# Moving layer 2's logits steps one chunk ahead in the bodies of layer 1

## The chip, the cores and the metric

The kernel runs on one core of one Trainium2 chip. The metric is the device time of one launch in microseconds (us). The kernel before takes 1067.36 us, the median of three runs (1065.39 to 1070.98).

## What is computed

Three stages follow each other: chunked attention, a mixture of experts with normalised logits (layer 1), and a second mixture with a skip score (layer 2). Every token goes to its best expert alone.

```python
def _moe_ref(x, expert_emb, tau, w1, w2):          # layer 1
    logits = normalised(x) @ normalised(expert_emb).T / tau
    expert_idx = argmax(logits, axis=1)
    gate_w = softmax(logits)[arange(N), expert_idx]
    for e in range(E):
        mask = expert_idx == e
        h = maximum(x[mask] @ w1[e], 0.0)
        out[mask] = gate_w[mask, None] * (h @ w2[e])

def _moe2_ref(x, w_skip, w_gate, w1, w2):          # layer 2
    do_compute = x @ w_skip > 0
    out = x.copy()
    xc = x[do_compute]
    logits = xc @ w_gate
    e_idx, gate_w = argmax(logits), softmax(logits) at the argmax
    y = the same experts' products on xc
    out[do_compute] = xc + y
```

There are 4608 tokens of 512 values, 8 experts and 1024 hidden values, all float32. The products are made of float32 values split in a high and a low part (fp32r): high times high, low times high, high times low.

## The kernel before

Attention (phase1) writes each token's row, with its gate and its number, to a place in DRAM sorted by expert. Layers 1 and 2 (moe) then run over these sorted rows. Their order is written out by hand, one instruction stream for each engine (functions sp, pe, act, dve, pool), and the engines meet at semaphores: take(e, s) waits until s has reached its count and counts it down again.

slots walks through the experts. A body works on one tile of rows: pair on 256 rows, single on 128, half on 64. The first body of an expert (first=True) is a pair in layer 1; it also converts the weights of the next expert: ScalarE casts a chunk of 512 KB to its high part (high, line 152), VectorE subtracts to the low part (split, line 155), and SP fetches the expert after that (fetch) into the staging tiles so freed. In layer 1 there are 18 pair bodies, eight of them firsts, and three bodies of single or half tiles; x < NE means layer 1.

A pair body on TensorE (pair in pe) has two products. Product one runs over eight chunks f of the hidden values; each chunk is 12 matmuls of 256 columns (line 795) into one of three PSUM tiles Hb and posts "h". ScalarE makes relu f out of it (HTh, line 1008, posts "hh"), VectorE the low half f (HTl, line 1212, posts "hl"). From the fourth chunk on TensorE waits for low half f - 3, whose tile Hb it writes again. Then TensorE transposes the next tile's X into XTp (xt, line 802), and product two runs in 16 steps of three matmuls of 512 columns into Yp; the first eight steps wait for the eight low halves in turn. ScalarE copies XTp to XTh, VectorE subtracts to XTl, SP loads the X after that, and ScalarE evicts Yp, scaled by the gate, into the tile y (yev).

The result y of a layer 1 body is the input of layer 2, so layer 2's logits are made from it inside the next body, in three steps between the chunks of product one (logits in pe). Step 0 waits for "yr" and transposes y into XTp (line 840, posts "yt"); ScalarE copies that to yT (line 984, posts "yT"). Step 1 multiplies yT with the gate's weights into a part of XTp (posts "lt"); ScalarE copies it to ls (line 986, posts "lS"). Step 2 sums the parts into lgp, again in XTp (posts "lg"). VectorE copies lgp to lgs (logits in dve, line 1105) and posts "lc". Since the transposes of the next X overwrite XTp, TensorE waits for lc ahead of them. "yr" is posted by VectorE's start of a body, which waits for "ys", the eviction of y by ScalarE, and copies the gate (line 1182). Behind f = 1 TensorE also makes the ranks (rk, line 192) of the tile whose logits were made a body before; ranked on VectorE reads them.

In the kernel before, TensorE's steps stand behind f = 2, 4 and 6, ScalarE's copies behind relu 2 and 4, and VectorE's copy behind low half 7. In first bodies ScalarE's casts stand behind relus 0, 1, 2, 3, 6 and 7 and at the body's end, and VectorE's splits behind low halves 1, 2, 3, 4 and 7 and after XTl.

Of the kernel before, what the change touches and what calls it, by code (L numbers as in the profile page):

```python
# [25 lines left out]
NE = 8  # L26
# [28 lines left out]
class Kernel:  # L55
# [556 lines left out]
    def moe(self, ctx):  # L612
# [178 lines left out]
        def pe(e):  # L791
# [69 lines left out]
            def pair(x, first=False):  # L861
                hi, lo = self.w[x % 2]
                begin(x, first)
                for f in range(KF):
                    if f >= 3:
                        e.wait_ge(sem["hl"], f - 2)
                    for i in range(3):
                        if f == 0 and i == 2:
                            take(e, "xl")
                        for k in range(KD):  # L870
                            r = mm(
                                Hb[f % 3][:, 0 : 2 * P].rearrange("p (a t) -> p a t", a=2), (hi, lo, hi)[i][:, k * FF + f * P : k * FF + (f + 1) * P],
                                (XTh, XTh, XTl)[i][:, k], i == 0 and k == 0, i == 2 and k == KD - 1,
                            )
                    r.then_inc(sem["h"], 1)
                    if f == 1 and x < NE and (x or not first):
                        rk()
                    if f in (2, 4, 6) and x < NE:
                        logits(f // 2 - 1)
                take(e, "xc")  # L880
                if x < NE:
                    take(e, "lc")
                xt()
                if first and x:
                    take(e, "wr2")
                mm2(x, 0, True)
                mm2(x, 1, False)
# [77 lines left out]
        def act(e):  # L965
            j = e.alloc_register("jac")
            s = nc.scalar

            def xh():
                take(e, "xt")  # L970
                s.copy(XTh, XTp).then_inc(sem["xh"], 1)

            highs = [0], [1], [2], [3], [], [], [4], [5], [6, 7]

            def high(x, r):
                if x <= LAST:
                    for c in r:
                        take(e, wf[c], 16)
                        self.split_hi(wcol(x, c)[0], c).then_inc(sem["wv"], 1)

            def logits(part):
                take(e, ("yt", "lt")[part])
                if part == 0:
                    s.copy(yT, XTp).then_inc(sem["yT"], 1)
                else:
                    s.copy(ls, lgq).then_inc(sem["lS"], 1)

            def rowcopy():
                take(e, "rf")
                s.copy(row[:, :, 0:DM], L[:, :, 0:DM]).then_inc(sem["rc"], 1)  # L990

            def expo():
                take(e, "nmx")
                for a in range(2):
                    s.activation(ex[:, a, :], lg[:, a, :], AF.Exp, bias=nm[:, a, :], accum_out=sm[:, a, :]).then_inc(
                        sem["sm"], 1
                    )

            def yev(a):
                take(e, "y")  # L1000
                r = s.activation(L[:, a, 0:DM], Yp[a], AF.Copy, scale=gt[:, a, :])  # L1001
                if a:
                    r.then_inc(sem["ys"], 1)

            def pair(x, first=False):
                for f in range(KF):
                    take(e, "h")
                    s.activation(HTh[:, f, :], Hb[f % 3][:, 0 : 2 * P], AF.Relu).then_inc(sem["hh"], 1)  # L1008
                    if f in (2, 4) and x < NE:
                        logits(f // 2 - 1)  # L1010
                    if first:
                        high(x + 1, highs[f])
                xh()
                if x < NE:
                    rowcopy()
                    expo()
                if first:
                    high(x + 1, highs[8])
                if x < NE:
                    e.drain()  # L1020
                    yev(0)
                    yev(1)

            def single(x, first=False, half=False):
                n = HP if half else P
                c = slice(0, n) if first else slice(P, P + n)
                if x < NE:
                    logits(0)
                if first:
                    high(x + 1, range(4))  # L1030
                for h in range(2):
                    take(e, "h")
                    s.activation(
                        Hs, Hb[h].rearrange("p (k f) -> p k f", k=4),
                        AF.Copy if half else AF.Relu,
                    ).then_inc(sem["r"], 1)
                    if h:
                        xh()
                    elif x < NE:
                        logits(1)  # L1040
                    take(e, "ht")
                    s.activation(
                        HTh[:, 4 * h : 4 * h + 4, c], (Hb[2], Hb[0])[h][:, 0 : 4 * n].rearrange("p (k f) -> p k f", k=4),
                        AF.Relu if half else AF.Copy,
                    ).then_inc(sem["hh"], 1)
                    if first and h:
                        high(x + 1, range(4, NCH))
                if x < NE:
                    rowcopy()
                    expo()  # L1050
                    e.drain()
                    if half:
                        take(e, "y")
                        s.activation(
                            L[0:HP, 1, 0:DM], Yp[1][0:HP, :], AF.Copy, scale=gt[0:HP, 1, :]
                        ).then_inc(sem["yb"], 1)
                    else:
                        yev(1)

            e.sem_inc(sem["ys"], 1)  # L1060
            for ph in range(2):
                expo()
                xh()
                slots(e, j, ph, pair, single, partial(single, half=True))
                if ph == 0:
                    for a in range(2):
                        take(e, "yt")
                        s.copy(yT[:, :, a, :], Hb[a].rearrange("p (k t) -> p k t", k=KD)).then_inc(sem["yT"], 1)

        def dve(e):  # L1070
# [145 lines left out]
            def pair(x, first=False):  # L1216
                start(x)
                for f in range(KF):
                    take(e, "hh")
                    low(f, Hb[f % 3][:, 0 : 2 * P])  # L1220
                    if f == 1 and x < NE and (x or not first):
                        ranked()
                    if first and f in (1, 2, 3, 4, 7):
                        split(e, x + 1, [min(f - 1, 4)])
                if x < NE:
                    logits()
                xl()
                if x < NE:
                    gating_a()
                    if first:  # L1230
                        split(e, x + 1, [5])
                    gating_b()
                    xc([1])
                    clear()
                    if first:
                        split(e, x + 1, [6, 7])
                else:
                    e.drain()
                    xc(range(2))
                    if first:  # L1240
                        split(e, x + 1, [5, 6, 7])
                    finals(range(2))

            def single(x, first=False, half=False):
# [5 lines left out]
                if x < NE:  # L1250
                    v.tensor_copy(t0[:, 0, :], self.bigi)
                    ranked()
                elif first:
                    split(e, x + 1, range(2))
                for h in range(2):
                    if h and x < NE:
                        logits()
                    take(e, "hh")
                    a = slice(4 * h, 4 * h + 4)
                    src, high = (Hb[2], Hb[0])[h][:, 0 : 4 * n].rearrange("p (k f) -> p k f", k=4), HTh[:, a, c].bitcast(F32)  # L1260
                    if half:
                        r = v.scalar_tensor_tensor(
                            HTh[:, a, o + HP : o + P], in0=src, scalar=0.0, in1=high, op0=ALU.max, op1=ALU.subtract
                        )
                    else:
                        r = v.tensor_tensor(HTl[:, a, c], src, high, op=ALU.subtract)
                    r.then_inc(sem["hl"], 4)
                    if h == 0 and first:
                        split(e, x + 1, range(2, 4))
# [148 lines left out]
```

## Time and profile before

| | before |
|---|---|
| median of 3 runs | 1067.36 us |
| profiled execution | 1066.52 us |
| its span | 1064.8 us |
| TensorE matmul, busy | 950.7 us (89%) |
| VectorE, busy | 539.6 us (51%) |
| ScalarE, busy | 478.4 us (45%) |
| GpSimd, busy | 196.1 us (18%) |
[...]

The span reaches from the first to the last instruction; attention takes its first 221 us, layer 1 the stretch to 778 us, and layer 2 the rest. A matmul's row lasts from its start to its modelled end, and matmuls overlap, so the time that one takes from the stream is read from start to start. The number in brackets at the end of a row is the time that the engine sat idle before it, and what ended that; PEq, ACTq and DVEq are the engines' own queues, which stand at a semaphore.

### The profile page before, as it was taken

How to read it: one execution, taken by the hardware profiler on the slowest of the kernel's cores; microseconds unless marked ns; L12 is line 12 of the kernel's file. 1: busy time of each engine (PE TensorE's matmuls, PEld its weight loads, DVE VectorE, ACT ScalarE, POOL GpSimd, SP SyncE). 2: the span in 40 equal slices, each digit the busy share in tenths (PEclk: the TensorE clock that was granted, in tenths of full speed). 3: DMA queues.
4: the chain of work that ended last, by engine and by line, in shares of the span. 5: the costliest groups of instructions: out<-in, count | busy, mean ns of one | idle time of the engine just before them, and what ended most of it. 6: DMA issues, size and time to landing. Idle time of an engine off the chain costs nothing. (4 is left out here: it accounts for less than half of the span.)

```text
span 1064.8 us, 20672 instructions
## 1 busy us (share of the span) xinstructions
PE 950.7 (89%) x7136; PEld 823.6 (77%) x7136; DVE 539.6 (51%) x1569; ACT 478.4 (45%) x931; POOL 196.1 (18%) x251
## 2 busy tenths in 40 slices
PE   7978999889999969999999999999999975979797
PEld 6866877678878858888788887788889864769685
DVE  5878889753226345343432244263255544646252
ACT  4767877643336535253433344363333423434241
POOL 4044442411111211111111111111121000000001
PEclk9999899999999998999999999999999988889899
DMA  8989998770153461405111511510525656572512
GB/s 211 254 241 238 246 229 204 259 258 22 40 198 106 171 199 48 171 36 193 52 41 41 197 47 42 203 46 21 197 64 208 212 171 220 174 249 91 192 47 65
DMA packets 133642, 157.11 MB, mean 148 GB/s; under 512 B 50421, under 2 KB 87285, under 8 KB 133232
## 3 DMA queue, kind: packets, MB, share of 16 engines
q1 hardware_dynamic: 121888, 132.16, 40.8%
q0 software_dynamic: 11600, 22.99, 5.9%
q8 instruction: 85, 1.39, 0.6%
q14 instruction: 69, 0.57, 0.2%
HBM read 123.42 MB, written 51.12 MB: 164 GB/s over the span
## 5 line engine op out<-in xcount | busy, mean ns | idle before, releaser
L795 PE MATMUL Yp<-w_hi,HTh 128*128 128x512 f32 x464 | 189.3, 408 | 0.0
L795 PE MATMUL Yp<-w_lo,HTh 128*128 128x512 f32 x464 | 186.2, 401 | 0.0
L1008 ACT ACTIVATE HTh<-Hb 128x256 fp32r<-128x256 f32 x208 | 79.9, 384 | 232.4 <-ACTq L660 230.1
L795 PE MATMUL Yp<-w_hi,HTl 128*128 128x512 f32 x440 | 176.5, 401 | 0.0
L1212 DVE SCALAR_TENSOR_TENSOR HTl<-Hb,HTh 128x256 fp32r<-128x256 f32 x208 | 87.6, 423 | 173.6 <-DVEq L660 173.5
L795 PE MATMUL Hb<-XTx,w_hi 128*128 128x256 f32 x832 | 141.1, 292 | 21.9 <-PEq L660 19.2
L155 DVE TENSOR_TENSOR w_lo<-stg,w_hi 128x1024 fp32r<-128x1024 f32 x120 | 143.6, 1216 | 0.5 <-DVEq L660 0.4
L795 PEld LDWEIGHTS Hb<-XTx,w_hi 128*128 128x128 f32 x832 | 115.6, 192 | 33.8 <-issue 26.0
L795 PE MATMUL Hb<-XTx,w_lo 128*128 128x256 f32 x832 | 133.1, 283 | 0.0
L152 ACT CAST w_hi<-stg 128x1024 fp32r<-128x1024 f32 x128 | 130.9, 1044 | 4.7 <-ACTq L660 4.7
L795 PE MATMUL Hb<-XTl,w_hi 128*128 128x256 f32 x832 | 132.8, 282 | 0.1
L1327 POOL DMA_INDIRECT xs<-row,few_i x44 | 44.9, 1020 | 466.9 <-POOLq L660 459.4
L1327 POOL DMA_INDIRECT out<-row,few_i x63 | 69.2, 1099 | 254.8 <-POOLq L660 239.1
L795 PEld LDWEIGHTS Hb<-XTx,w_lo 128*128 128x128 f32 x832 | 114.1, 191 | 0.0
L795 PEld LDWEIGHTS Hb<-XTl,w_hi 128*128 128x128 f32 x832 | 113.6, 191 | 0.5 <-issue 0.5
L795 PEld LDWEIGHTS Yp<-w_hi,HTh 128*128 128x128 f32 x464 | 89.3, 192 | 20.0
L795 PEld LDWEIGHTS Yp<-w_lo,HTh 128*128 128x128 f32 x464 | 89.2, 192 | 20.0
L795 PEld LDWEIGHTS Yp<-w_hi,HTl 128*128 128x128 f32 x440 | 84.4, 192 | 20.4
L1001 ACT ACTIVATE y<-Yp,few_f 128x512 f32<-128x512 f32 x37 | 25.5, 688 | 113.4 <-ACTq L660 113.4
L1182 DVE COPY few_f<-few_f 128x2 f32<-128x2 f32 x32 | 5.8, 182 | 137.5 <-DVEq L660 110.9
L1093 DVE TENSOR_TENSOR XTl<-XTp,XTx 128x1024 fp32r<-128x1024 f32 x34 | 41.6, 1223 | 59.7 <-DVEq L660 59.6
L802 PE MATMUL XTp<-ident,X 128*128 128x128 f32 x272 | 37.4, 282 | 36.3 <-PEq L660 36.1
(207 smaller groups left out, 1311.0 us busy)
## 6 DMA issues: line engine op xcount, KB each, us to landing
stg<-in_moe_w SPq DMA_DIRECT2D x128, 512.0 KB, 6.5
X<-xs SPq DMA_DIRECT2D x34, 516.0 KB, 3.8
vbd<-in_v SPq DMA_DIRECT2D x144, 64.0 KB, 4.5
xs<-pad SPq DMA_DIRECT2D x16, 516.0 KB, 10.9
qs<-in_q SPq DMA_DIRECT2D x12, 512.0 KB, 5.0
ks<-in_k SPq DMA_DIRECT2D x12, 512.0 KB, 8.0
y<-xs SPq DMA_DIRECT2D x11, 512.0 KB, 4.2
xs<-pads SPq DMA_DIRECT2D x16, 258.0 KB, 4.6
```

The source lines that it names most:

```text
L152: return self.nc.scalar.copy(hi, self.stg[c % NSTG])
L155: return eng.tensor_tensor(lo, self.stg[c % NSTG], hi.bitcast(F32), op=ALU.subtract)
L795: return nc.tensor.matmul(out, lhsT=l, rhs=r, start=start, stop=stop)
L802: r = nc.tensor.transpose(XTp[:, k, a, :], X[:, a, k * P : (k + 1) * P], ident)
L1001: r = s.activation(L[:, a, 0:DM], Yp[a], AF.Copy, scale=gt[:, a, :])
L1008: s.activation(HTh[:, f, :], Hb[f % 3][:, 0 : 2 * P], AF.Relu).then_inc(sem["hh"], 1)
L1093: v.tensor_tensor(XTl, XTp, XTh.bitcast(F32), op=ALU.subtract).then_inc(sem["xl"], 1)
L1182: r = v.tensor_copy(gt, gtn)
L1212: v.scalar_tensor_tensor(HTl[:, f, :], in0=src, scalar=0.0, in1=HTh[:, f, :].bitcast(F32), op0=ALU.max, op1=ALU.subtract).then_inc(sem["hl ...
L1327: e.indirect_dma_start(out=dst, out_offset=bass.IndirectOffsetOnAxis(ap=idx, axis=0), in_=src, in_offset=None, bounds_check=bound - 1, oob ...
```

## The change

The three steps on TensorE move from behind f = 2, 4 and 6 to behind f = 1, 3 and 5 of product one; in f = 1 step 0 follows the ranks. ScalarE's two copies move from behind relus 2 and 4 to behind relus 1 and 3, ahead of the weight cast that stands there in first bodies. VectorE's copy moves from behind low half 7 to ahead of low half 6 in pairs. In single and half bodies VectorE's copy moves from between the two low halves to ahead of the first. No instruction is added or removed.

```diff
@@ pair in pe
                     if f == 1 and x < NE and (x or not first):
                         rk()
-                    if f in (2, 4, 6) and x < NE:
-                        logits(f // 2 - 1)
+                    if f in (1, 3, 5) and x < NE:
+                        logits(f // 2)
                 take(e, "xc")
@@ pair in act
                     s.activation(HTh[:, f, :], Hb[f % 3][:, 0 : 2 * P], AF.Relu).then_inc(sem["hh"], 1)
-                    if f in (2, 4) and x < NE:
-                        logits(f // 2 - 1)
+                    if f in (1, 3) and x < NE:
+                        logits(f // 2)
                     if first:
                         high(x + 1, highs[f])
@@ pair in dve
                 for f in range(KF):
+                    if f == KF - 2 and x < NE:
+                        logits()
                     take(e, "hh")
                     low(f, Hb[f % 3][:, 0 : 2 * P])
...
-                if x < NE:
-                    logits()
                 xl()
@@ single in dve
+                if x < NE:
+                    logits()
                 for h in range(2):
-                    if h and x < NE:
-                        logits()
                     take(e, "hh")
```

## Rows read from the trace of the kernel before

**Rows 1.** The page's first part: busy us (share of the span) and instructions, TensorE.

```profile
PE 950.7 (89%) x7136; PEld 823.6 (77%) x7136; DVE 539.6 (51%) x1569; ACT 478.4 (45%) x931; POOL 196.1 (18%) x251
```

**Rows 2.** Waits of TensorE, 221 to 778 us: line, releaser, total us, times, longest.

```profile
PE XTp L802 <- PEq L660: 35.4, 18, 2.6
PE Hb L795 <- PEq L660: 5.5, 1, 5.5
```

**Rows 3.** Timeline, end of product one, second body of an expert: start us, length us, instruction.

```profile
265.46 0.63 PE L795 MATMUL Hb<-XTl,w_hi 128*128 128x256 f32 x4
...
266.74 0.42 DVE L1212 SCALAR_TENSOR_TENSOR HTl<-Hb,HTh 128x256 fp32r<-128x256 f32 x1 [1.43 <-DVEq L660]
267.08 0.17 DVE L1105 COPY lgs<-XTp 128x18 f32<-128x18 f32 x1
...
267.55 1.07 PE L802 MATMUL XTp<-ident,X 128*128 128x128 f32 x8 [1.46 <-PEq L660]
```

**Rows 4.** Timeline, the same place in the first body of an expert.

```profile
377.44 0.63 PE L795 MATMUL Hb<-XTl,w_hi 128*128 128x256 f32 x4
...
379.06 1.22 DVE L155 TENSOR_TENSOR w_lo<-stg,w_hi 128x1024 fp32r<-128x1024 f32 x1
380.19 0.17 DVE L1105 COPY lgs<-XTp 128x18 f32<-128x18 f32 x1
...
380.66 1.06 PE L802 MATMUL XTp<-ident,X 128*128 128x128 f32 x8 [2.59 <-PEq L660]
```

**Rows 5.** Timeline of TensorE, the same place in a pair body of layer 2.

```profile
824.39 0.64 PE L795 MATMUL Hb<-XTl,w_hi 128*128 128x256 f32 x4
824.87 1.03 PE L802 MATMUL XTp<-ident,X 128*128 128x128 f32 x8
```

**Rows 6.** Timeline, product one of the body of rows 3: gate copy, ranks, logits steps.

```profile
253.51 0.17 DVE L1182 COPY few_f<-few_f 128x2 f32<-128x2 f32 x1 [5.68 <-DVEq L660]
...
255.23 0.19 PE L192 MATMUL Rp<-oh,ones 128*128 128x8 bf16 x2
...
260.58 0.64 PE L795 MATMUL XTp<-yT,wg 128*32 128x256 f32 x8
...
261.36 0.37 ACT L986 COPY yT<-XTp 128x256 f32<-128x256 f32 x1 [0.21 <-ACTq L660]
...
264.08 0.51 PE L795 MATMUL XTp<-sel,yT 128*128 128x9 f32 x4
```

**Rows 7.** Timeline, start of the body behind a half tile: gate copy and ranks.

```profile
322.48 0.17 DVE L1182 COPY few_f<-few_f 128x2 f32<-128x2 f32 x1 [0.20 <-DVEq L660]
...
323.31 0.19 PE L192 MATMUL Rp<-oh,ones 128*128 128x8 bf16 x2
```

**Rows 8.** Timeline of ScalarE in the first body of rows 4, behind relu 2.

```profile
369.97 1.02 ACT L984 COPY yT<-XTp 128x1024 f32<-128x1024 f32 x1 [0.48 <-ACTq L660]
370.88 1.05 ACT L152 CAST w_hi<-stg 128x1024 fp32r<-128x1024 f32 x1
371.83 0.38 ACT L1008 ACTIVATE HTh<-Hb 128x256 fp32r<-128x256 f32 x1
```

**Rows 9.** Loads of X: one issue on SP's timeline; issue to landing of 23 loads.

```profile
390.31 0.38 SPq L726 DMA_DIRECT2D X<-xs  x1
...
DMA to landing us min/median/max: 3.4/3.8/6.4
```

**Rows 10.** Windows of 12 us behind the wait: us, PE busy (matmuls), granted clock, DMA share, GB/s.

```profile
238.60:250.60 12.00, 11.94 (x49) 0.86 0.16 46
336.70:348.70 12.00, 11.95 (x56) 1.00 0.58 217
...
267.50:279.50 12.00, 11.95 (x56) 1.00 0.17 44
```

**Rows 11.** Timeline of TensorE, start of the expert behind one with a single body.

```profile
398.41 1.19 PE L795 MATMUL Hb<-XTx,w_hi 128*128 128x256 f32 x4 [5.47 <-PEq L660]
```

## The prediction

> (f counts the chunks of product one, its relus and its low halves from 0 to 7, as the code does.)
>
> **What bounds the kernel now.** I read the page's busy shares first, then who waited for whom on TensorE over layer 1, then the timeline of single bodies. TensorE is busy 89% of the span [rows 1]; no other engine passes 51% on the same page. Between 221 and 778 us, which is all of layer 1, TensorE has only two waits of weight: 35.4 us in 18 waits ahead of the transposes of the next X (line 802), and one of 5.5 us at the start of a product [rows 2]. Elsewhere in layer 1 its matmuls stand end to end. So a wait of TensorE that goes shortens the time, and a step on ScalarE or VectorE costs only what it makes TensorE wait.
>
> The 18 waits are one per pair body, and come in two sizes. In a body that isn't the first of its expert, the last four matmuls of product one start at 265.46. VectorE takes the last low half at 266.74, copies the logits at 267.08, and the transposes start at 267.55, 0.30 us after that copy ends (267.08 + 0.17) [rows 3]. In the first body of an expert a weight split of 1.22 us stands between low half and copy; the copy comes at 380.19, and the transposes at 380.66, again 0.30 us after its end [rows 4]. The releaser is in both cases "lc", which the logits copy posts: the transposes overwrite XTp, in which the logits stand. There are eight firsts (one per expert) and ten others: 8 x 2.6 + 10 x 1.46 = 35.4, which is the row of waits.
>
> **The change part by part.**
>
> *VectorE's copy moves from behind low half 7 (in firsts, also behind its split) to ahead of low half 6.* This takes relu 7, low half 7 and the split out of the chain that ends in lc. What remains for the transposes is xf (the next X in SBUF), xc and lc. A case with the first two alone is layer 2: its pair bodies have no logits, and there the transposes start 0.48 us after the last four matmuls start (824.39 to 824.87), with no wait [rows 5]. Against that spacing, the others lose 267.55 - 265.46 - 0.48 = 1.61 us each, the firsts 380.66 - 377.44 - 0.48 = 2.74 us. If lc is early: 10 x 1.61 + 8 x 2.74 = 16.1 + 21.9 = 38.0 us.
>
> *Is lc early?* The last logits matmuls now run behind f = 5, two chunks before the end of product one; a chunk is three runs of four matmuls at 0.48 [rows 5], so 1.4 us, and two are 2.8. Low half 5 should trail the end of its chunk as low half 7 does: that starts at 266.74 where the chunk's end is 265.46 + 0.48 = 265.94, so it ends (0.42 long) 1.2 us behind. The copy and its 0.30 of signal add 0.5: lc stands 1.7 us after f = 5, over 1 us before f = 7 ends. That is the cover in the others; in firsts the splits make VectorE run later or earlier by about half a microsecond. If it were gone, TensorE would wait in line 802 as now, by the difference. Low halves 6 and 7 slip by at most 0.17 us; product two needs low half 7 only at the eighth of its sixteen steps, some 5 of 12 us after the transposes begin [rows 10].
>
> *TensorE's transposes of y move ahead by a chunk.* They wait for "yr", posted by VectorE at the body's start behind the last eviction of the body before. The gate copy that posts it starts at 253.51 and ends at 253.68; TensorE is through the ranks at 255.42, where the transposes will stand [rows 6]. Margin 1.7, less 0.3 of signal: 1.4 us. The tightest body is that behind a half tile: copy at 322.48, ranks until 323.50 [rows 7], margin 0.5. I take 0; were the margin exceeded, everything in TensorE's queue would stand behind the wait.
>
> *ScalarE's two copies move with them*: yT at 1.0 us, ls at 0.37 [rows 6, 8]. The three steps stay two chunks apart, so TensorE finds yT and ls as early as now. In firsts the yT copy now stands between relu 1 and the cast of weight chunk 1, so relu 2 comes late: the pattern today is copy 369.97, cast 370.88, relu 371.83 [rows 8], which I put at half a microsecond's lag of relu 3, and the same lag would fall on relu 2. TensorE needs low half 2 before f = 5: two chunks of 1.4 and the logits matmuls of 0.6 [rows 6] after f = 2 ends, 3.4 us, against the usual 1.2 and the lag of 0.5. Cover 1.7 us; VectorE's split between is over by then, since it waits for relu 2 too. I take 0, with 0.5 x 8 = 4 us as bound.
>
> [...]
>
> *Single and half bodies* (three in layer 1): VectorE's logits copy goes ahead of low half 0 and swaps some 0.4 with 0.17 us beside TensorE's second half of product one; 0, with bounds of 0.4 each to both sides, 1.2 us in all. No DMA is moved, and neither SP's nor POOL's order changes. *X is there in time*: a load that SP issues as late as 390.31, behind the weight fetches, lands in 6.4 us at the longest [rows 9], before the body that needs it for its transposes even begins (398.41) [rows 11].
>
> *The clock.* In five of the eight firsts TensorE's granted clock falls after the wait: 0.86 over the 12 us behind it, against 1.00 in the other three firsts and behind the others' waits [rows 10]. [...] A fall costs 0.14 x 12 = 1.7 us by that row, or 7 matmuls fewer of 56, 7 / 56 x 12 = 1.5; I take 1.6, five are 8.0 us. With the wait gone I expect the falls gone: none stands behind a wait of 1.46, nor behind layer 2's transposes, which don't wait. Bounds 0 and 8.0.
>
> [...]
>
> The wait of 5.47 us at 398.41 [rows 11] stands at an expert's start, behind an expert with one body; no moved step releases it, and I leave it as it is.
>
> **Sum.** 38.0 + 8.0 = 46.0 us. The profiled execution took 1066.52 (span 1064.8), so 1020.5; the median shown is 0.84 higher, which gives 1021.4. I say 1021.
>
> **The rivals.**
> *The clock is not given back* (other short waits still let it fall): 38.0 alone, 1029.
> *A part of the wait stays in firsts*, because VectorE or ScalarE is late there: about a split of 1.22 us still ahead of lc, or relu 2 holding f = 5. 8 x 1.22 = 9.8 us less gives 1031; with the clock's falls kept too, 1039.
> *The wait only changes its name*: xf or xc ends as late as lc does now, and the time stays 1067. For it: lc hides what comes just before it. Against it: layer 2 waits there for nothing [rows 5], and X lands over 10 us early.
> *Slower*: yr takes the place of lc. TensorE's order is fixed, so each microsecond by which yr comes late behind f = 1 costs 18, and beyond 46.0 / 18 = 2.6 us per body the change loses; at 3.6 us it would be 1067 + 18 = 1085. It decides from 1.4 + 2.6 = 4.0 us later than the row shows. Against it: the gate copy follows ScalarE's eviction, which no moved step touches.
>
> **Chances.** Forecast 0.63; clock kept 0.17; part of the wait stays 0.14; no change 0.03; slower 0.03. Faster by over 0.5% (5.3 us, about what a measurement of this kernel can tell from no change) holds the first three: 0.94; within 0.5% 0.03; slower 0.03. The range: 1016 at the low end (the forecast less a scatter of 2 as the runs shown have it, the 1.2 of the singles, and 2 should the wait of 5.47 shrink); 1032 at the high end takes in the kept clock and the 1031.
>
> **What would show it.** Right: no wait at line 802 in layer 1, transposes 0.48 us behind the last four matmuls; the logits copy on VectorE between low halves 5 and 6, over 1 us before product one ends; bodies of the others 1.6 us shorter; clock 1.00 behind each first. Wrong: a wait of TensorE at the transposes of y (yr), at the first matmuls of f = 5 in firsts (low half 2), or still at line 802 with another releaser; or new falls of the clock.

## The result and the profile after

The changed kernel takes 1019.88 us (median of four runs, 1017.32 to 1023.73) where the kernel before takes 1067.95 (four runs): a ratio of 0.957, with a 95% interval of 0.953 to 0.960, or 48 us less. The profiled execution of after took 1023.73 us, the slowest of its four; its span is 1022.0 us against 1064.8.

The page's busy line of after, and the waits of TensorE from 215 to 760 us, which is layer 1 with its two ends (line, releaser, total us, times, longest):

```profile
PE 935.7 (92%) x7136; PEld 812.5 (79%) x7136; DVE 539.8 (53%) x1569; ACT 478.6 (47%) x931; POOL 198.4 (19%) x251
```

```profile
PE Hb L795 <- PEq L660: 6.8, 2, 6.3
PE XTp L802 <- PEq L660: 3.6, 3, 1.9
```

The instructions are the same in number. TensorE's busy time fell by 15 us with no work taken away; a part of that is the matmuls behind five firsts: over 12 us the granted clock was 0.86 there before, with 49 matmuls, and is 1.00 now, with 56 to 59. The 35.4 us of [rows 2] are 3.6 us. Of these three waits one stands ahead of layer 1's first body (1.4) and one in layer 2 (0.3); the only one left in a body of layer 1 is 1.93 us in the very first.

The second body of an expert, where [rows 3] stood (timeline, all engines):

```profile
260.77 0.51 PE L795 MATMUL XTp<-sel,yT 128*128 128x9 f32 x4
...
261.58 0.42 DVE L1212 SCALAR_TENSOR_TENSOR HTl<-Hb,HTh 128x256 fp32r<-128x256 f32 x1 [0.97 <-DVEq L660]
...
261.92 0.17 DVE L1105 COPY lgs<-XTp 128x18 f32<-128x18 f32 x1
```

```profile
263.55 0.63 PE L795 MATMUL Hb<-XTl,w_hi 128*128 128x256 f32 x4
264.02 0.71 PE L802 MATMUL XTp<-ident,X 128*128 128x128 f32 x5
```

The copy stands behind low half 5 and ends at 262.09; with the 0.30 us of signal of [rows 3] lc is there at 262.4, 1.6 us before the transposes, which follow the last four matmuls by 0.47 us. The first body of an expert, where [rows 4] stood:

```profile
367.52 0.42 DVE L1212 SCALAR_TENSOR_TENSOR HTl<-Hb,HTh 128x256 fp32r<-128x256 f32 x1 [0.25 <-DVEq L660]
...
367.86 0.17 DVE L1105 COPY lgs<-XTp 128x18 f32<-128x18 f32 x1
...
369.08 0.63 PE L795 MATMUL Hb<-XTl,w_hi 128*128 128x256 f32 x4
...
369.56 1.03 PE L802 MATMUL XTp<-ident,X 128*128 128x128 f32 x8
...
370.37 0.42 DVE L1212 SCALAR_TENSOR_TENSOR HTl<-Hb,HTh 128x256 fp32r<-128x256 f32 x1 [0.98 <-DVEq L660]
...
370.71 1.22 DVE L155 TENSOR_TENSOR w_lo<-stg,w_hi 128x1024 fp32r<-128x1024 f32 x1
```

Low half 7 and the split still run when they ran before against the end of product one; they now stand beside the transposes, where nobody waits for them. The clock behind the firsts' transposes of X, in windows of 12 us as in [rows 10] (us, TensorE busy (matmuls), granted clock, DMA share, GB/s); three of the eight, the others read the same:

```profile
238.40:250.40 12.00, 11.97 (x56) 1.00 0.17 46
...
403.30:415.30 12.00, 12.00 (x58) 1.00 0.57 201
454.40:466.40 12.00, 12.00 (x58) 1.00 0.57 204
```

Behind these transposes no first of layer 1 has a fall of the clock any more in this execution. From the first transposes at line 802 to the last ones of layer 1 it is 503.74 us (220.02 to 723.76) against 549.32 before (219.58 to 768.90): 45.6 us less. The rest of the profiled span gave 2.3 us back: 298.2 against 295.9 us from the last transposes of layer 1 on. There the waits ahead of three starts of experts are about as long as before (7.26, 6.03 and 6.04 us before, 7.48, 6.53 and 5.86 now), but the clock came back later behind them in this execution: in the last 2.0 to 2.4 us of the windows below it was 0.98, 0.74 and 0.58 before, and 0.50 in all three after. The same three places (windows as above), before and after:

```profile
867.60:873.00 5.40, 5.36 (x34) 0.71 0.03 9
952.30:957.00 4.70, 4.69 (x25) 0.60 0.05 17
1006.90:1011.00 4.10, 4.08 (x10) 0.54 0.03 6
```

```profile
822.70:828.00 5.30, 5.28 (x25) 0.50 0.02 5
908.20:913.00 4.80, 4.79 (x22) 0.50 0.04 13
963.60:968.00 4.40, 4.40 (x11) 0.50 0.03 6
```

No moved step is near these, and the profiled execution is 3.9 us above the median of its kernel. Two kernels measured later, whose layer 2 has the same instructions, take 293.1 and 297.1 us for the same stretch in their profiled executions (changed again, two fetches later), so the 2.3 us lie within the scatter of this stretch.

### The profile page after: what moved, and what is told of

It reads as the page before. It is cut to its first block, busy times and chain, and to the rows that moved or that the text cites. A ratio compares the mean times of both kernels' runs of the same rounds, so it can differ in the third digit from the quotient of the medians.

```text
span 1022.0 us, 20672 instructions
## 1 busy us (share of the span) xinstructions
PE 935.7 (92%) x7136; PEld 812.5 (79%) x7136; DVE 539.8 (53%) x1569; ACT 478.6 (47%) x931; POOL 198.4 (19%) x251
## 5 line engine op out<-in xcount | busy, mean ns | idle before, releaser
L795 PE MATMUL Yp<-w_hi,HTh 128*128 128x512 f32 x464 | 186.1, 401 | 0.0
L795 PE MATMUL Yp<-w_lo,HTh 128*128 128x512 f32 x464 | 183.4, 395 | 0.0
L795 PE MATMUL Yp<-w_hi,HTl 128*128 128x512 f32 x440 | 174.1, 396 | 0.0
L795 PEld LDWEIGHTS Hb<-XTx,w_hi 128*128 128x128 f32 x832 | 116.7, 194 | 35.4 <-issue 27.2
L1327 POOL DMA_INDIRECT xs<-row,few_i x44 | 49.9, 1134 | 419.2 <-POOLq L660 411.8
L1327 POOL DMA_INDIRECT out<-row,few_i x63 | 66.6, 1057 | 257.2 <-POOLq L660 241.5
L331 PE MATMUL sc<-kbd,qT 128*64 128x128 f32 x576 | 39.7, 280 | 6.7 <-ACT kbd L321 5.6
```

The costliest lines, as they stand in the source:

```text
L331: nc.tensor.matmul(sc4[64 * cc : 64 * cc + 64, hp, :], lhsT=qT[:, hp, c, :], rhs=kb[:, hp, c, :], start=True, stop=True,)
L795: return nc.tensor.matmul(out, lhsT=l, rhs=r, start=start, stop=stop)
L1327: e.indirect_dma_start(out=dst, out_offset=bass.IndirectOffsetOnAxis(ap=idx, axis=0), in_=src, in_offset=None, bounds_check=bound - 1, oob ...
```

## The experiments

The kernels were measured in three groups, each on one chip with runs of the kernel before beside them. In the first group that took 1065.63 us, in the second 1078.79, in the third 1077.64, with attention ending some 11 us later in the profiled kernels of these two. Times of different groups are compared by their ratios alone.

### VectorE's copy alone

Against the kernel before; TensorE's and ScalarE's steps stay where they were.

```diff
                 for f in range(KF):
+                    if f == KF - 2 and x < NE:
+                        logits()
                     take(e, "hh")
...
-                if x < NE:
-                    logits()
                 xl()
```

> The kernel before with VectorE's logits copy in pairs ahead of low half 6, and nothing else moved: TensorE's steps stay behind f = 2, 4, 6, ScalarE's copies behind relus 2 and 4. Theory (the wait was the chain relu 7, low half 7, split, copy): the last logits matmuls stand behind f = 6, the copy follows some 0.6 us after, lc some 1.0 us after f = 6, and a chunk is 1.4 us, so all waits at line 802 go but that of the very first body; 1021 to 1024 us, at most some 2 us above the changed kernel. Rival (the steps on TensorE and ScalarE had to move, too): waits of 0.5 us or more stay in most of 18 bodies, 1030 us or more.

It took 1019.57 us, ratio 0.956 (0.951 to 0.961): as fast as the whole change, a little below what was expected. The waits at line 802, 217 to 735 us, and the end of product one in a second body (timeline):

```profile
PE XTp L802 <- PEq L660: 3.6, 2, 2.5
```

```profile
262.51 0.51 PE L795 MATMUL XTp<-sel,yT 128*128 128x9 f32 x4
...
263.17 0.18 DVE L1105 COPY lgs<-XTp 128x18 f32<-128x18 f32 x1 [0.84 <-DVEq L660]
263.32 0.42 DVE L1212 SCALAR_TENSOR_TENSOR HTl<-Hb,HTh 128x256 fp32r<-128x256 f32 x1
...
264.36 1.03 PE L802 MATMUL XTp<-ident,X 128*128 128x128 f32 x8
```

Of the two waits one (1.2 us) stands ahead of the first body of layer 1, the other (2.47) in the very first body; the other 17 are gone, as expected. VectorE now stands 0.84 us at the head of its queue for lg, since the last logits matmuls come only behind f = 6. That costs nothing, because it had stood idle there anyway: low half 6 starts 0.81 us after these logits matmuls, as before. The copy ends 1.0 us before the transposes. So the wait was the place of this one copy of 18 columns, behind low half 7, and the steps on TensorE and ScalarE didn't have to move. From the transposes of X in one body to those in the next it is 25.66 us here (430.17 to 455.83) against 25.56 with the whole change (428.92 to 454.48): the steps' place is worth 0.1 us a body, some 2 us in all, which the time of four runs can't tell.

### TensorE's and ScalarE's steps alone

```diff
-                    if f in (2, 4, 6) and x < NE:
-                        logits(f // 2 - 1)
+                    if f in (1, 3, 5) and x < NE:
+                        logits(f // 2)
...
-                    if f in (2, 4) and x < NE:
-                        logits(f // 2 - 1)
+                    if f in (1, 3) and x < NE:
+                        logits(f // 2)
```

> The kernel before with TensorE's steps behind f = 1, 3, 5 and ScalarE's copies behind relus 1 and 3, VectorE's copy where it was. Theory: 18 waits of 1.46 and 2.6 us at line 802 as before, 35 us in all; 1064 to 1068 us. Rival (the steps' place brings a good part): below 1055.

1064.74 us, ratio 1.000 (0.997 to 1.003). The waits at line 802, 217 to 735 us:

```profile
PE XTp L802 <- PEq L660: 33.1, 17, 2.6
```

One of them, 0.6 us, stands ahead of the first body, and two of 1.46 us come after 735 us; so there are 18 in bodies, as before. Making the logits earlier without copying them earlier leaves every wait in its place: the time of this chain is set by its last link. The clock fell in four of the eight firsts here (0.86 over 12 us), in the same places as before but for the last (at 712.73 it stayed at 1.00).

### The copy behind low half 7, ahead of the split

Against the changed kernel: what the firsts have more than the others goes, what all have stays.

```diff
-                    if f == KF - 2 and x < NE:
-                        logits()
                     take(e, "hh")
                     low(f, Hb[f % 3][:, 0 : 2 * P])
+                    if f == KF - 1 and x < NE:
+                        logits()
```

> The changed kernel with VectorE's copy in pairs behind low half 7 and ahead of the split there. Theory: 18 waits at line 802, all of about 1.46 us, 26 us in all, and no fall of the granted clock behind the firsts, since none stood behind a wait of 1.46 before: 1020 + 18 x 1.6 = 1049. Rival (the falls come in firsts whatever the wait): clock 0.86 behind about five firsts again, 1057.

1047.04 us, ratio 0.981 (0.976 to 0.987). 17 of the 18 waits are 1.46 to 1.55 us; the very first body keeps 2.62. Windows behind that one and behind two of the other seven firsts:

```profile
237.80:249.80 12.00, 11.93 (x49) 0.86 0.14 46
334.50:346.50 12.00, 11.99 (x56) 1.00 0.59 219
...
411.70:423.70 12.00, 11.99 (x56) 1.00 0.59 216
```

The time is a little below the expected 1049, and the expectation missed the wait that stayed. Here the clock fell behind the one long wait, and behind none of the seven that had become short, at the same places in the program: four of them had fallen before (the first at 411.70 had 0.86 with its wait of 2.59 before, and has 1.00 here). In this run the fall goes with the long wait of 2.62 us (0.86 behind it), not with first bodies (1.00 behind the seven waits of 1.46 to 1.55).

### The steps two chunks ahead

```diff
-                    if f in (1, 3, 5) and x < NE:
+                    if f in (0, 2, 4) and x < NE:
...
-                    if f in (1, 3) and x < NE:
+                    if f in (0, 2) and x < NE:
```

> The changed kernel with TensorE's steps behind f = 0, 2, 4 and ScalarE's copies behind relus 0 and 2. Theory (yr is the next bound): yr stands about 1.65 us after a body's first matmul, chunk 0 ends at 1.4, so TensorE waits at line 840 for 0.2 to 0.4 us in some 14 bodies and for a microsecond behind the half tile, and has one switch of matmul kind more; 1024 to 1028. Rival (yr is never near): no wait at line 840, 1018 to 1022.

1026.99 us, ratio 0.964 (0.959 to 0.969). The time is in the expected range, but the waits are not as they were expected. All waits at line 840 in layer 1, and the start of a second body:

```profile
PE XTp L840 <- PEq L660: 2.0, 4, 0.8
```

```profile
254.67 0.63 PE L795 MATMUL Hb<-XTl,w_hi 128*128 128x256 f32 x4
254.92 0.17 DVE L1182 COPY few_f<-few_f 128x2 f32<-128x2 f32 x1 [5.37 <-DVEq L660]
...
255.23 1.07 PE L840 MATMUL XTp<-ident,y 128*128 128x128 f32 x8
```

yr's copy ends at 255.09, and the transposes of y start 0.14 us later; the chunk's next matmul could have stood at 255.14 (254.67 + 0.47). So yr costs 0.1 us in a usual body, not 0.2 to 0.4: its signal is shorter than the 0.30 I had taken over from lc. Of the four waits the two of any size stand behind the two half tiles, 0.81 us each; the other two (0.2) stand in the half tiles' own bodies, as in the changed kernel. A body is 25.73 us long against 25.55, 3 us over some 17 bodies, and in the very first body the clock fell behind its wait of 1.93 us (0.86 over 240.00 to 252.00, where the changed kernel has 1.00), 1.6 us more by the prediction's estimate of a fall; with the half tiles' 1.6 this is 6 of the 7 us that layer 1 is longer. The bound that the slower rival named is thus real, and lies one chunk ahead of where the change put the step.

### Single and half bodies as before

```diff
-                if x < NE:
-                    logits()
                 for h in range(2):
+                    if h and x < NE:
+                        logits()
                     take(e, "hh")
```

> The changed kernel with VectorE's copy in single and half bodies back between the two low halves. Theory: the three single and half bodies neither gain nor lose by its place; 1020, and transposes at line 802 in these three within 0.4 us of where the changed kernel has them. Rival: the part in singles is worth 1 us or more.

Ratio 0.958 (0.954 to 0.961) in the second group. From the transposes of y to those of X a half body takes 6.44 us here and 6.45 in the changed kernel. In the single body it is 6.96 us (354.05 to 361.01) against 6.71 (342.26 to 348.97): behind the low half lc comes 0.25 us late. The body behind it is 0.16 us shorter here (20.43 against 20.59), so this part is worth 0.1 us, within the 0.4 expected and too little for the time to show.

### The very first body: which signal is left

Two kernels ask for the releaser of the one wait that stayed. In the changed kernel SP issues the load of X at 234.39 and it lands 3.9 us later, at 238.3:

```profile
234.39 0.43 SPq L726 DMA_DIRECT2D X<-xs  x1
234.62 0.17 DVE L1105 COPY lgs<-XTp 128x18 f32<-128x18 f32 x1
...
238.43 1.06 PE L802 MATMUL XTp<-ident,X 128*128 128x128 f32 x8 [1.93 <-PEq L660]
```

The transposes start 0.14 us behind that landing, over 3 us after lc. In three kernels of the first group (copy alone, copy ahead of the split, steps two chunks ahead), where this wait is 2.47, 2.62 and 1.93 us, they start 0.1 to 0.2 us behind the landing, too. The load stands behind the padding rows, for whose landing SP waits; it issues them at 227.22, behind a wait for POOL's scatters, the last of which POOL issues at 218.14. They land 6.8 us later, while the last four weight fetches, issued from 220.82 to 222.4, are under way, too: these take 7.7 to 11.0 us to land.

All six remaining fetches behind the padding rows:

```diff
-                if ph == 0:
-                    fetch(1, range(2, NSTG))
                 take(e, "pl")
...
                 padrows(order[0])
+                if ph == 0:
+                    fetch(1, range(2, NSTG))
```

> The changed kernel with SP's first six remaining weight fetches of expert 1 issued behind the first rows of padding, in place of ahead of them. The one wait left at line 802 in layer 1 is 1.9 us in the very first body. Theory: its releaser is the load of X, which SP issues at 234.4 behind the padding rows, which land late beside the weight fetches; with these behind, the load is early and the wait goes; 1018. Rival: another releaser (lc or xc) holds the transposes there, the wait stays, 1020; or the weights now come late and ScalarE's casts hold relus, above 1020.

Ratio 0.957 (0.953 to 0.960), no change; the wait grew:

```profile
243.10 1.05 ACT L152 CAST w_hi<-stg 128x1024 fp32r<-128x1024 f32 x1 [2.36 <-ACTq L660]
...
251.94 1.30 PE L802 MATMUL XTp<-ident,X 128*128 128x128 f32 x5 [3.21 <-PEq L660]
```

SP issued the load of X 2.1 us earlier than in the kernel with the single bodies as before, of the same group (244.15 against 246.25), but it is now issued behind 3 MB of weights (six fetches of 512 KB from 238.91 on); the transposes start 7.8 us behind its issue, against 4.0 in that kernel (246.25 to 250.21), and a cast waited 2.36 us. Its landing isn't recorded, so this run alone doesn't say whether xf is the releaser. The theory, that the wait goes, failed; it had left out what the load itself stands behind.

So only the last two fetches, whose casts come at the end of the body, behind the load:

```diff
                 if ph == 0:
-                    fetch(1, range(2, NSTG))
+                    fetch(1, range(2, 6))
...
                         load(ph, second[x], between=ahead)
+                        if ph == 0:
+                            fetch(1, range(6, NSTG))
```

> The changed kernel as it is, to stand beside the next one on the same chip. All theories: the ratio of its first measurement, 0.957; one wait of 1.9 to 2.3 us at line 802 in the very first body.

> The changed kernel with only the last two weight fetches of expert 1 (chunks 6 and 7) moved behind the second load of X on SP; the four ahead stay. Theory: in the very first body the transposes wait for xf alone; the padding rows queue behind weights, so with 1 MB less ahead of them they land some 2 us earlier, the load of X is issued some 2 us earlier, and the wait of 1.9 us shrinks to 0.3 or less; casts 6 and 7 stand only at the end of the body and still find their chunks. 1.5 to 2 us below the changed kernel beside it, 3 if a fall of the clock goes with the wait. Rival (the padding rows wait for the scatters of POOL and not for weights): the load is issued as late as now, the wait stays at 1.9 or more, and the time is the same.

The changed kernel took 1034.07 us (ratio 0.960, 0.957 to 0.963; its wait, 2.54 us, is above the expected 1.9 to 2.3), this one 1029.61 (0.955, 0.952 to 0.959). The load and the transposes, first of the changed kernel, then of this one:

```profile
246.37 0.43 SPq L726 DMA_DIRECT2D X<-xs  x1
...
250.33 1.94 PE L802 MATMUL XTp<-ident,X 128*128 128x128 f32 x8 [2.54 <-PEq L660]
```

```profile
243.91 0.43 SPq L726 DMA_DIRECT2D X<-xs  x1
...
247.83 1.07 PE L804 MATMUL XTp<-ident,X 128*128 128x128 f32 x8 [0.24 <-PEq L660]
```

The load goes out 2.5 us earlier, the transposes follow it by 3.9 us in both, and the wait is 0.24; the fall of the clock behind it (transposes of 1.94 us, and 0.86 over 250.30 to 262.30) went too (1.07 us, and 1.00 over 248.00 to 260.00). So xf holds the transposes in the very first body. The theory of the queue holds: SP issues the padding rows no earlier than in the changed kernel (239.18 against 238.87), but the load behind them 2.5 us earlier. That the kernel is faster by 4.5 us at the medians, where 3 were expected with a fall, rests on six runs each whose intervals overlap; the 2.3 us of wait and the fall account for 4 of them, and the two profiled executions take the same time, since the stretch behind layer 1 is 4 us longer in this one (297.1 against 293.1).

## Why the prediction was right

The forecast was 1021, the range 1016 to 1032; measured is 1019.88. By its steps:

*The chain that ends in lc*: right. Taking the copy out from behind relu 7, low half 7 and the split took the wait away, and nothing else did (the copy alone 0.956, the steps alone 1.000). The spacing of [rows 5] that I borrowed from layer 2 is what layer 1 now has, 0.47 to 0.48 us.

*10 x 1.61 + 8 x 2.74 = 38.0*: right in sum, by luck, with two kinds of terms off (measured: 17.4 of the others, 20.1 of seven firsts and 0.7). The others gained more: a body is 25.55 us (264.02 to 289.57) where it was 27.31 (267.55 to 294.86), and over the five that no fall touches the gain is 1.74, of which the copy alone brings 1.65. The 0.09 is the steps' place, which I had taken at 0. The likely reason, not tried by itself, is that the transposes of y now stand right behind the ranks, so that TensorE changes between kinds of matmuls once less: the first four matmuls behind the ranks took 0.56 us from start to start before (255.28 to 255.84), where the next four take 0.47 (255.84 to 256.31). And one first, the very first body, gained not 2.74: from transposes to transposes it is 18.41 us against 19.08, 0.7 less. The step that failed is "X is there in time". I showed the issue of one load, in an expert's later course [rows 9], and took it for all. In the very first body before the change:

```profile
234.67 0.43 SPq L726 DMA_DIRECT2D X<-xs  x1
...
238.14 0.17 DVE L1105 COPY lgs<-XTp 128x18 f32<-128x18 f32 x1
...
238.66 1.39 PE L802 MATMUL XTp<-ident,X 128*128 128x128 f32 x8 [2.64 <-PEq L660]
```

The load's 3.9 us end at 238.6, just where lc came (238.14 + 0.17 + 0.30). There the wait had two causes, and the rival "the wait only changes its name" held in one body of 18.

*lc's cover*: put at over 1 us; 1.6 in the others, and 1.2 in firsts (copy's end 368.03 and 0.30 against 369.56).

*ScalarE's copies*: taken at 0, with 4 us as bound. In the first body after the change:

```profile
360.21 1.01 ACT L984 COPY yT<-XTp 128x1024 f32<-128x1024 f32 x1 [0.67 <-ACTq L660]
361.12 1.05 ACT L152 CAST w_hi<-stg 128x1024 fp32r<-128x1024 f32 x1
362.07 0.39 ACT L1008 ACTIVATE HTh<-Hb 128x256 fp32r<-128x256 f32 x1
```

relu 2 stands behind copy and cast (362.07 behind 360.21 and 361.12), as forecast. Low half 2 ends at 363.0, 1.9 us before f = 5 starts (364.90), where the cover was put at 1.7; TensorE waits nowhere for it, so the 0 was right.

*yr*: no wait of over 0.2 us at line 840 in the bodies of layer 1; cover as forecast behind the half tile, where the gate copy ends at 317.32 and the transposes start at 318.04. One chunk further ahead it is used up.

*The clock*: 8.0 us expected back, and all five falls are gone (0.86 before, 1.00 now), which gave 7.7 (the five bodies with a fall gained 3.29 on average, the others 1.74). That they hang on the wait was argued in the prediction, and is shown by the copy ahead of the split (1.00 behind seven firsts with short waits, four of which had 0.86 before).

*The wait at the expert with one body*: left as it is, 5.47 before and 6.35 after; layer 1 gave 0.9 back there. Its cause stays open.

Sum over layer 1: 17.4 of the others, 20.1 of seven firsts (2.87 each in the four that nothing else touches), 0.7 of the very first, 7.7 of the clock's five falls and -0.9 is 45.0; measured 45.6. The medians differ by 48.1, 2.5 us more than measured in layer 1; the scatter of either kernel's runs (5.6 and 6.4 us from lowest to highest) covers that.

## What to carry to other kernels

Where an engine waits for a buffer, look at what the releasing instruction stands behind in its own queue, and not only at when its data are ready: here the data were there a chunk earlier, and a copy of 0.17 us stood behind a relu, a low half and a split that it had nothing to do with. Put the instruction that frees a buffer ahead of work that nobody waits for yet, even if its engine then stands idle for it. And before counting a wait as gone in all its places, look in each for the signal that comes second, above all in the first round, where the loads are on another schedule: here X landed in the very first body only 0.1 us before the transposes.

## What the runs showed of the hardware

The granted clock fell behind waits at line 802 of 2.47 to 2.64 us in some places and not in others at the same length (five of eight before, four of the same eight with the steps alone, so that seven places agree). In the kernel before it stood at 0.50 for some 3 us at each fall (at the first one 0.50 from 240.00 to 242.00, and 1.00 from 243.00 to 245.00), and over 12 us it was 0.86. At 1.93 us it fell in the kernel with the steps two chunks ahead (0.86 over 12 us) and not in the changed kernel (1.00), and not at 2.27 us in the kernel with the single bodies as before (1.00); behind the short waits of 1.45 to 1.55 us it never fell (1.00), in 37 places of three kernels (before, steps alone, copy ahead of the split). In these runs the 1.6 us that I had estimated for a fall therefore hang on more than the wait's length; what decides between waits of the same length stays open. Where the wait was gone, at seven firsts of the changed kernel and of the copy alone, the clock was 1.00 over the 12 us behind the transposes.

From the end of VectorE's copy to TensorE's matmul it took 0.30 us at lc (267.25 to 267.55 in the kernel before) and 0.14 us at yr (255.09 to 255.23 with the steps two chunks ahead); I had used the first for both. The code has a likely reason, not tried by itself: behind lc TensorE still takes xf ahead of the transposes, behind yr it takes nothing more, and where xf came last, in the very first body, the transposes start 0.14 us behind the landing.
